# First inverse FFT step in parts of 32 rows by 64 columns, with a scratch layout ordered by k1

## The chip, the cores and the metric

The kernel runs on one core of a Trainium2 chip. Its time is the device time of one execution in microseconds. Three runs of the kernel before gave 374.64, 375.82 and 376.35 us, with a median of 375.82 us. The profiled execution took 376.04 us; its trace, from the first to the last instruction, spans 374.1 us.

Five engines run side by side, each working through its own instructions in order: TensorE (PE, matrix products; PEld is its weight load), VectorE (DVE), ScalarE (ACT), GpSimd (POOL) and SyncE (SP, which here only issues DMA transfers). DMA transfers are issued from SP, ACT and POOL and are carried by 16 DMA engines.

## The reference

The input has 2048 positions (S) of 448 channels (D). The result is a sum of three terms: the input, a gated long convolution, and a two-layer MLP.

```python
xn = layernorm(q)
k_shift = causal depthwise conv of k with 4 taps
kv = k_shift * v
y  = irfft(rfft(kv, 2S) * rfft(ssm_k, 2S))[:S] + kv * ssm_D   # a causal convolution of length S per channel
A  = xn * y
B  = mish(xn @ w1 + b1) @ w2                                   # 448 -> 1792 -> 448
out = q + A + B
```

## The kernel before

**Two strands on one PE.** The MLP and the convolution share every engine. The host code is a list of 116 slots. Each slot holds a piece of the MLP: even slots a first-layer group (`g1_mm`, L462, pairs of 128 hidden units for a chunk of 256 positions), odd slots the Mish and the split of its result into two parts (`mish`, L470, L73, L74) and a second-layer group (`g2_mm`, L487 to L489). The parts of the convolution are put into slots by hand: `at(slot, ...)` places a piece ahead of the slot's MLP work, `after(slot, ...)` behind it. No scheduler moves anything afterwards, so this list is the order on every engine.

**The convolution as products.** Each channel's 2048 samples are written as n = n2 + 32 n1, with 32 values of n2 and 64 of n1. A forward transform is one product over n1 (`f1_mm`, L124, result to the scratch tensors `Dh` and `Dkv` in DRAM) and one over n2 (`f2_mm`, L198). The 64 values of k1, the index that goes with n1, are treated in eight octets `o`; within one, k1 is given by t (4 values) and r (2 values). Per octet the spectra are multiplied on DVE (`prod`, L231, result `ya` real and `yc` imaginary). The first inverse step (`i1_mm`, L243) takes k2 back to n2: for each (t, r) the 32 rows of k2, real (c = 0) and imaginary (c = 1), are multiplied by the constant `gi`, with the two c summed in PSUM. `i1_out` copies the two PSUM tiles to `qe` on ACT (L251) and stores `qe` to the DRAM scratch `E` (L255, from SP). An octet comes every third slot from slot 69 to slot 90.

**The second inverse step.** It works on chunks of positions. `e_load(c)` (L278) brings chunk c of `E` into a tile `e` of 128 partitions, for the two halves h of k1 (octets 0 to 3 and 4 to 7). `fold(c)` forms the sum `ex` and the difference of the halves on DVE (L283, L285), `i2_mm(c)` (L301) takes k1 back to n1, and `gate` multiplies by the normalised input. Chunks 6 and 7 come first: their loads are issued from SP, at slot 94, their folds stand behind slot 95, their products ahead of slot 98. The loads of the other six chunks are issued from POOL. Four buffers hold `e`, so the loads of chunks 2 to 5 wait until an earlier chunk's product has read its buffer.

**Tiles of the PE.** All convolution products use parts of the 128 by 128 array: f1 has 32 rows by 64 columns, f2 64 by 32, i1 32 by 32 and i2 64 by 32. Each of these float32 products shows in the trace as two weight loads and two matmuls.

Of the kernel before, what the change touches and what calls it, by code (L numbers as in the profile page):

```python
# [7 lines left out]
F32 = mybir.dt.float32  # L8
# [6 lines left out]
S, D, F = 2048, 448, 1792  # L15
# [4 lines left out]
NCHUNK = S // CH  # L20
# [8 lines left out]
I2_AT = {98: (6, 7), 102: (0, 1), 106: (2, 3), 109: (4, 5)}  # L29
# [6 lines left out]
def tile_kernel(ctx: ExitStack, tc, q, k, v, sk, hT, sD, w1, b1, w2, c_f1, c_g, c_gi, c_i2, out):  # L36
    nc = tc.nc
    V = nc.vector

    def pool(name, bufs=1, stack=ctx, **kw):  # L40
        return stack.enter_context(tc.tile_pool(name=name, bufs=bufs, **kw))
# [7 lines left out]
    dp = pool("scratch", space=DRAM)  # L49
# [2 lines left out]

    Dh = dp.tile([NO * 16, 32, D], F32, name="Dh")
    Dkv = dp.tile([NO * 16, 32, D], F32, name="Dkv")
    E = dp.tile([2, 2, 32, 2, NCHUNK, 2, D], F32, name="E")

    f1id = cp.tile([128, 2, 128], F32, name="f1id")
    f1, ident = f1id[:, 0], f1id[:, 1]
# [17 lines left out]
    def pc():  # L76
        return pcp.tile([128, 2, 512], F32, name="pc")
# [93 lines left out]
    GT, AH, AV, HS, PV, Y = {}, {}, {}, {}, {}, {}  # L171

    def t2(shape, name, bufs=1):
        if not sp2:
            ph1.close()
            sp2.append(ph2.enter_context(tc.tile_pool(name="ph2", bufs=1, reuse_waits="tile")))
        return sp2[0].tile(shape, F32, name=name, bufs=bufs)
# [56 lines left out]
    def i1_mm(o):  # L234
        gi = GT[o][1]
        ps = [pc(), pc()]
        for c in range(2):
            for t in range(4):
                ts = slice(32 * t, 32 * t + 32)
                for r in range(2):  # L240
                    for jj in range(2):
                        cg = 64 * jj + 32 * r
                        nc.tensor.matmul(ps[t // 2][cg:cg + 32, t % 2, :D], gi[ts, r, c, 32 * jj:32 * jj + 32],  # L243
                                         Y[o][c][ts, r], start=c == 0, stop=c == 1, tile_position=(32 * t, cg))
        PS["I", o] = ps
        Y.pop(o)

    def i1_out(o):
        qe = t2([128, 4, D], "qe")
        for i, p in enumerate(PS.pop(("I", o))):  # L250
            nc.scalar.copy(qe[:, 2 * i:2 * i + 2], p[:, :, :D])  # L251
        k = 8 * (o % 4)
        for jj in range(2):
            dst = E[o // 4, jj, k:k + 8].rearrange("(t r) m j b d -> (r m j b) t d", t=4)
            nc.sync.dma_start(dst, qe[64 * jj:64 * jj + 64])  # L255


    ph3 = ExitStack()
# [3 lines left out]
    def t3(shape, name, bufs=2):  # L262
        if not sp3:
            ph2.close()
            sp3.append(ph3.enter_context(tc.tile_pool(name="ph3", bufs=2, reuse_waits="tile")))
            i2 = sp3[0].tile([128, 2, 32], F32, name="i2", bufs=1)
            nc.sync.dma_start(i2, c_i2)
            sp3.append(i2)
        return sp3[0].tile(shape, F32, name=name, bufs=bufs)
# [4 lines left out]
    def e_load(c):  # L274

        e = EE[c] = t3([128, 2, 2, D], "e3", 4)
        src = E[:, :, :, :, c].rearrange("h j k m b d -> (j k m) h (b d)")
        (nc.sync if c in I2_AT[min(I2_AT)] else nc.gpsimd).dma_start(e.rearrange("p h b d -> p h (b d)"), src)  # L278

    def fold(c):  # L280
        e = EE[c]
# [267 lines left out]
    for g, t in enumerate(KV_AT):  # L549
        d = t - (KV_AT[g - 1] if g else t - 6)  # L550
# [16 lines left out]
    for o in range(NO):  # L567
        s, d = OCT_AT[0] + OCT_AT[1] * o, OCT_AT[1]
        h = s - 1 if o else H0_AT
        at(h - d if o else h - 2, o_load, AH, Dh, o, "ah")  # L570
        at(s - d if o else s - 2, o_load, AV, Dkv, o, "av")
        at(h, h2_mm, o)
        after(h, h2_out, o)
        at(s, v2_mm, o)
        after(s, v2_out, o)
        at(s, gi_load, o)
        after(s + 1, prod, o, 0)
        after(s + 2, prod, o, 1)
        at(s + 4, i1_mm, o)
        after(s + 4, i1_out, o)  # L580

    ts = sorted(I2_AT)
    for n, t in enumerate(ts):
        for m, c in enumerate(I2_AT[t]):
            at(ts[n - 2] + 1 if n > 1 else ts[0] - 4 + n, e_load, c)
            at(ts[n - 1] + (2 if m else -2 if n == 2 else -1) if n > 1 else ts[0] - 5 + m, qa_load, c)
            after(t - 3, fold, c)
            at(t, i2_mm, c)
            after(t, gate, c)
            at(t + 2 + m, gate_out, c)  # L590
# [30 lines left out]
    ps = [g2p.tile([128, 512], F32, name="pg2") for _ in range(2)]  # L621
# [11 lines left out]
    for s in range(nslots):  # L633
        j = s // 2 - G2_LAG - 1
# [11 lines left out]
def _constants():  # L646
    import numpy as np

    w = lambda e: np.exp(-2j * np.pi * (np.asarray(e) % 8192) / 8192.0)

    n1 = np.arange(64)
    k1 = np.arange(64)
    W = w(32 * n1[:, None] * (4 * k1[None, :] - 1))

    W = W.reshape(32, 2, 64).transpose(1, 0, 2).reshape(64, 64)
    Wo = W.reshape(64, 8, 2, 4).transpose(0, 1, 3, 2)
    f1 = np.stack([Wo.real, Wo.imag], axis=4).reshape(64, 128)
    f1 = np.concatenate([f1, f1])

    i2 = np.stack([W.real.T, W.imag.T], axis=1)[:32].reshape(4, 2, 4, 2, 64).transpose(0, 2, 1, 3, 4).reshape(64, 2, 32) / 2048  # L660
    i2 = np.concatenate([i2, i2])
    n2 = np.arange(32)[:, None] // 2 + 16 * (np.arange(32)[:, None] % 2)
    k2 = np.arange(32)[None, :]
    G = np.zeros((2, 2, 32, 8, 4, 2, 32))
    GI = np.zeros((4, 32, 8, 2, 2, 2, 2, 8, 2))
    for kk in range(64):
        o, r, t = kk // 8, kk // 4 % 2, kk % 4
        g = w(n2 * (4 * kk - 1) + 256 * n2 * k2)
        G[r, 0, :, o, t, 0], G[r, 1, :, o, t, 0] = g.real, -g.imag
        G[r, 0, :, o, t, 1], G[r, 1, :, o, t, 1] = g.imag, g.real  # L670

        gt = g.T.reshape(32, 8, 2, 2).transpose(0, 2, 1, 3)
        GI[t, :, o, r, 0, :, 0], GI[t, :, o, r, 1, :, 0] = gt.real, gt.imag
        GI[t, :, o, r, 0, :, 1], GI[t, :, o, r, 1, :, 1] = -gt.imag, gt.real
    c = lambda a: np.ascontiguousarray(a, dtype=np.float32)
    return dict(c_f1=c(np.stack([f1, np.eye(128)], axis=1)), c_g=c(G.reshape(128, 8, 4, 2, 32)), c_gi=c(GI.reshape(128, 8, 2, 2, 64)),
                c_i2=c(i2))
# [27 lines left out]
```

## Time and profile before

| | |
|---|---|
| profiled execution | 376.04 us, span 374.1 us |
| PE busy | 366.6 us, 98% of the span |
| DVE, ACT, POOL busy | 266.1, 177.4, 23.1 us |
| i1 products (L243) | 512 matmuls, two for each product |
| stores of `E` (L255, SP) | 16 of 448 KB, median 5.5 us to landing |
| loads of `e` (L278) | 2 of 896 KB from SP, 6 from POOL |
| granted PE clock | 1.00 in nearly all stretches |

Busy time of a matmul group is that of overlapping records, so the length of a PE piece is better read from the start of its first matmul to the start of the next group. Idle time is put down to the engine or transfer that ended it. A trace row's first number is the start in us from the beginning of the span, the second its length.

### The profile page before, as it was taken

Reading aid. Unit: us, or ns where it says so; the run is one execution under the profiler, and the core shown is the slowest. Engines: PE = TensorE matmul, PEld = TensorE weight load, DVE = VectorE, ACT = ScalarE, POOL = GpSimd, SP = SyncE. Lnnn points to the kernel's source line nnn. Section 1 sums busy time; section 2 is a strip of 40 time slices with the busy share of each in tenths; the row PEclk is TensorE's granted clock in tenths of the full one; section 3 lists DMA queues with packets and bytes.
Section 4 is the critical chain, followed back from the end, with each engine's and each line's share of the span. In section 5 each row is a group of like instructions: output and inputs, shape, how many; then the busy total and the mean of one; then the engine's idle time right before and its main releaser. Section 6 shows DMA issues by size and latency. Waiting matters only on the chain.

```text
span 374.1 us, 7973 instructions
## 1 busy us (share of the span) xinstructions
PE 366.6 (98%) x3392; PEld 295.6 (79%) x3392; DVE 266.1 (71%) x356; ACT 177.4 (47%) x298; POOL 23.1 (6%) x40
## 2 busy tenths in 40 slices
PE   8999999999999999999999999999999999999995
PEld 3887888888888988988886666666666889789884
DVE  5798758999999998996444746754664823797841
ACT  4777553542436333533454745556555436135450
POOL 2010001000020001000000000110000011102110
PEclk9999999999999999999999999999999999999999
DMA  8899979747587436604794598879394459839973
GB/s 283 296 314 324 390 284 271 182 157 224 156 271 217 98 86 212 197 2 123 236 298 152 145 299 228 261 240 263 110 296 145 116 129 330 304 112 279 230 139 90
DMA packets 32099, 79.38 MB, mean 212 GB/s; under 512 B 2881, under 2 KB 18114, under 8 KB 32066
## 3 DMA queue, kind: packets, MB, share of 16 engines
q1 hardware_dynamic: 25442, 55.56, 46.3%
q10 hardware_dynamic: 4896, 15.08, 14.8%
q0 software_dynamic: 1728, 8.26, 8.3%
q8 instruction: 26, 0.43, 0.4%
q14 instruction: 7, 0.06, 0.1%
HBM read 50.44 MB, written 28.44 MB: 211 GB/s over the span
## 4 chain that ended last, share of the span: by engine, by line
PE 80%; DVE 9%; DMA 5%; ACT 3%; issue 2%; POOL 0%; SPq 0%; ACTq 0%; DVEq 0%
PE pg L462 32%; PE pg L487 10%; PE pg L488 10%; PE pg L489 10%; PE pc L198 7%; PE pc L243 4%; PE pc L124 3%; PE pc L301 2%; PE pg L423 2%; DMA kr<-in_k_dram 2%; DMA Dkv<-st 1%; DMA av<-Dkv 1%; DVE st L131 1%; DVE bst L379 1%; DVE acl L74 1%
## 5 line engine op out<-in xcount | busy, mean ns | idle before, releaser
L470 ACT ACTIVATE a<-pg,b1t 128x256 f32<-128x256 f32 x112 | 47.2, 473 | 108.7 <-PE pg L462 90.1
L462 PE MATMUL pg<-XH,w1h 128*128 128x256 f32 x448 | 91.2, 285 | 0.3 <-DVE XL L433 0.2
L487 PE MATMUL pg<-w2h,ach 128*128 128x448 f32 x224 | 83.6, 373 | 0.2 <-DVE qt L494 0.2
L462 PEld LDWEIGHTS pg<-XH,w1h 128*128 128x128 f32 x448 | 69.7, 188 | 17.5 <-issue 14.4
L488 PE MATMUL pg<-w2l,ach 128*128 128x448 f32 x224 | 81.3, 363 | 0.4 <-DVE w2l L74 0.4
L489 PE MATMUL pg<-w2h,acl 128*128 128x448 f32 x224 | 81.3, 363 | 0.0
L74 DVE TENSOR_TENSOR acl<-a,ach 128x512 fp32r<-128x512 f32 x56 | 38.5, 687 | 57.9 <-ACT ach L73 57.6
L462 PE MATMUL pg<-XL,w1h 128*128 128x256 f32 x448 | 69.7, 277 | 0.0
L462 PEld LDWEIGHTS pg<-XL,w1h 128*128 128x128 f32 x448 | 59.5, 188 | 0.1
L462 PE MATMUL pg<-XH,w1l 128*128 128x256 f32 x336 | 56.9, 278 | 0.0
L487 PEld LDWEIGHTS pg<-w2h,ach 128*128 128x128 f32 x224 | 42.0, 187 | 14.1 <-issue 11.2
L462 PEld LDWEIGHTS pg<-XH,w1l 128*128 128x128 f32 x336 | 47.0, 188 | 0.0
L488 PEld LDWEIGHTS pg<-w2l,ach 128*128 128x128 f32 x224 | 42.1, 188 | 3.0 <-DVE w2l L74 0.7
L489 PEld LDWEIGHTS pg<-w2h,acl 128*128 128x128 f32 x224 | 42.1, 188 | 2.7
L73 ACT CAST ach<-a 128x512 fp32r<-128x512 f32 x56 | 34.9, 623 | 1.8
L162 DVE TENSOR_TENSOR x<-x 128x896 f32<-128x896 f32 x24 | 26.2, 1091 | 0.8
L435 ACT CAST XH<-pg 128x512 fp32r<-128x512 f32 x16 | 9.4, 589 | 28.0 <-PE pg L423 28.0
L433 DVE TENSOR_TENSOR XL<-pg,XH 128x512 fp32r<-128x512 f32 x16 | 10.9, 685 | 14.9 <-ACT XH L435 14.8
L130 ACT COPY st<-pc 128x896 f32<-128x896 f32 x16 | 14.5, 908 | 13.3 <-PE pc L124 13.3
L131 DVE TENSOR_TENSOR st<-pc,st 128x896 f32<-128x896 f32 x16 | 17.4, 1086 | 4.5 <-ACT st L130 4.1
L251 ACT COPY qe<-pc 128x896 f32<-128x896 f32 x16 | 13.7, 911 | 13.4 <-PE pc L243 13.4
L390 POOL TENSOR_TENSOR shift<-mv,mone 128x2 f32<-128x2 f32 x7 | 2.8, 394 | 281.0 <-DVE mv L382 281.0
(65 smaller groups left out, 397.0 us busy)
## 6 DMA issues: line engine op xcount, KB each, us to landing
Dh<-st ACTq DMA_DIRECT2D x16, 448.0 KB, 5.5
Dkv<-st ACTq DMA_DIRECT2D x16, 448.0 KB, 4.9
ah<-Dh SPq DMA_DIRECT2D x8, 896.0 KB, 7.1
av<-Dkv SPq DMA_DIRECT2D x8, 896.0 KB, 6.1
E<-qe SPq DMA_DIRECT2D x16, 448.0 KB, 5.5
e<-E POOLq DMA_DIRECT2D x6, 896.0 KB, 8.4
kr<-in_k_dram SPq DMA_DIRECT2D x10, 448.0 KB, 6.1
x<-in_hT_dram SPq DMA_DIRECT2D x8, 448.0 KB, 6.8
```

The costliest lines, as they stand in the source:

```text
L73: nc.scalar.copy(h, raw)
L74: V.tensor_sub(l, raw, h)
L130: nc.scalar.copy(st[:, 1], o)
L131: V.tensor_add(st[:, 0], e, st[:, 1])
L162: V.tensor_add(KV[g], KV[g], o)
L198: nc.tensor.matmul(p[32 * t:32 * t + 32, r, :D], g[rs, t, c], a[rs, t], start=True, stop=True, tile_position=(64 * r, 32 * t))
L243: nc.tensor.matmul(ps[t // 2][cg:cg + 32, t % 2, :D], gi[ts, r, c, 32 * jj:32 * jj + 32], Y[o][c][ts, r], start=c == 0, stop=c == 1, tile_ ...
L462: nc.tensor.matmul(ps[:, n], l, r, start=n_ == 0, stop=n_ == len(mm) - 1)
L470: nc.scalar.activation(a[:, n], ps[:, n], AF.Mish, bias=b1t[:, 2 * p + n:2 * p + n + 1])
L487: nc.tensor.matmul(ps, ah[:, n, cs], w2h[:, f], start=f == 0, stop=False)
L488: nc.tensor.matmul(ps, ah[:, n, cs], w2l[:, f], start=False, stop=False)
L489: nc.tensor.matmul(ps, al[:, n, cs], w2h[:, f], start=False, stop=f == NF - 1)
```

## The change

Five places change. `E` gets the order (half h, 32 values of k1, m for real and imaginary part of the result, j for even and odd n2, chunk, b, channel) in place of (h, j, k1, m, chunk, b, channel). The constant `gi` has its 64 columns in the order (m, j, chunk, b) in place of (j, m, chunk, b). `i1_mm` makes one product of 64 columns where it made two of 32, so an octet has 16 products in place of 32, and the output partitions are grouped by r alone. `i1_out` still makes two stores of 448 KB for an octet; each now takes all 128 partitions of `qe` for two values of t, where it took 64 partitions for all four. `e_load` makes two loads of 448 KB, one for each half h, where it made one of 896 KB. On the DRAM side such a load has 2 values of j on the outside and then 64 rows of 3584 B; on the on-chip side it has 128 partitions of 3584 B. Before, both sides had 128 on the outside.

```diff
-    E = dp.tile([2, 2, 32, 2, NCHUNK, 2, D], F32, name="E")
+    E = dp.tile([2, 32, 2, 2, NCHUNK, 2, D], F32, name="E")
...
             for t in range(4):
                 ts = slice(32 * t, 32 * t + 32)
                 for r in range(2):
-                    for jj in range(2):
-                        cg = 64 * jj + 32 * r
-                        nc.tensor.matmul(ps[t // 2][cg:cg + 32, t % 2, :D], gi[ts, r, c, 32 * jj:32 * jj + 32],
-                                         Y[o][c][ts, r], start=c == 0, stop=c == 1, tile_position=(32 * t, cg))
+                    nc.tensor.matmul(ps[t // 2][64 * r:64 * r + 64, t % 2, :D], gi[ts, r, c], Y[o][c][ts, r],
+                                     start=c == 0, stop=c == 1, tile_position=(32 * t, 64 * r))
...
-        for jj in range(2):
-            dst = E[o // 4, jj, k:k + 8].rearrange("(t r) m j b d -> (r m j b) t d", t=4)
-            nc.sync.dma_start(dst, qe[64 * jj:64 * jj + 64])
+        dst = E[o // 4, k:k + 8].rearrange("(t r) m j c b d -> (r m j c b) t d", t=4)
+        for i in range(2):
+            nc.sync.dma_start(dst[:, 2 * i:2 * i + 2], qe[:, 2 * i:2 * i + 2])
...
-        src = E[:, :, :, :, c].rearrange("h j k m b d -> (j k m) h (b d)")
-        (nc.sync if c in I2_AT[min(I2_AT)] else nc.gpsimd).dma_start(e.rearrange("p h b d -> p h (b d)"), src)
+        src = E[:, :, :, :, c].rearrange("h k m j b d -> h j (k m) (b d)")
+        for h in range(2):
+            (nc.sync if c in I2_AT[min(I2_AT)] else nc.gpsimd).dma_start(e[:, h].rearrange("p b d -> p (b d)"), src[h])
...
-        GI[t, :, o, r, 0, :, 0], GI[t, :, o, r, 1, :, 0] = gt.real, gt.imag
-        GI[t, :, o, r, 0, :, 1], GI[t, :, o, r, 1, :, 1] = -gt.imag, gt.real
+        GI[t, :, o, r, 0, 0], GI[t, :, o, r, 1, 0] = gt.real, gt.imag
+        GI[t, :, o, r, 0, 1], GI[t, :, o, r, 1, 1] = -gt.imag, gt.real
```

The changed kernel's line numbers are two lower from `i1_mm` on (L243 is L241) and one lower from the loads of `e` on (L278 is L277).

On PE, the first octet's inverse step (slot 69) stands between a first-layer and a second-layer group. Before:

```order
L462 MATMUL pg_2342<-XL,w1h 128x256 x4
L243 MATMUL pc<-ya,gi 32x448 x16
L243 MATMUL pc<-yc,gi 32x448 x16
L487 MATMUL pg_2067<-w2h,ach 128x448
L488 MATMUL pg_2067<-w2l,ach 128x448
```

With the change (a row's size is output partitions by columns, its count is of products):

```order
L461 MATMUL pg_2342<-XL,w1h 128x256 x4
L241 MATMUL pc<-ya,gi 64x448 x8
L241 MATMUL pc<-yc,gi 64x448 x8
L486 MATMUL pg_2067<-w2h,ach 128x448
L487 MATMUL pg_2067<-w2l,ach 128x448
```

The place is the same, with half as many products, each twice as wide in its output.

On SP, the stores of the last octet (`E<-qe`) are followed by the constant of the second inverse step, the input of a chunk, and the loads of chunks 6 and 7. Before:

```order
L255 DMA E<-qe 64x4x448 x2
L267 DMA i_3607<-in_c_i_dram 128x64
L292 DMA q_3609<-in_q_dram 128x896
L278 DMA e_3630<-E 128x2x896
L278 DMA e_3632<-E 128x2x896
L292 DMA q_3634<-in_q_dram 128x896
```

With the change:

```order
L253 DMA E<-qe 128x2x448 x2
L265 DMA i_3479<-in_c_i_dram 128x64
L291 DMA q_3481<-in_q_dram 128x896
L277 DMA e_3502<-E 128x1x896 x2
L277 DMA e_3505<-E 128x1x896 x2
L291 DMA q_3508<-in_q_dram 128x896
```

Each of the two loads has become two of half the size in the same place; the size shown is that of the on-chip side.

On DVE, whose order has not changed, the folds of chunks 6 and 7 stand between two splits of MLP results (`acl`):

```order
L74 TENSOR_TENSOR acl<-a,ach 128x512
L282 TENSOR_TENSOR ex<-e_3502 128x896
L284 TENSOR_TENSOR e_3502<-e_3502 128x896
L282 TENSOR_TENSOR ex<-e_3505 128x896
L284 TENSOR_TENSOR e_3505<-e_3505 128x896
L432 TENSOR_TENSOR XL<-pg_3576,XH 128x4x128
L74 TENSOR_TENSOR acl<-a,ach 128x512
```

What stands behind them is a part of the next chunk's MLP input (`XL`) and the next split, which wait on DVE until the folds have been done.

## Prediction

> **What bounds the kernel now.** I read the page's busy times and the chain that ended last, then the list of waits, then the timeline around the places that the change touches.
>
> ```profile
> PE 366.6 (98%) x3392; PEld 295.6 (79%) x3392; DVE 266.1 (71%) x356; ACT 177.4 (47%) x298; POOL 23.1 (6%) x40
> PE 80%; DVE 9%; DMA 5%; ACT 3%; issue 2%; POOL 0%; SPq 0%; ACTq 0%; DVEq 0%
> ```
>
> The PE is busy for 98% of the span and makes up 80% of the chain: PE time saved is time saved, and whatever stops the PE is added in full. Its waits on the second inverse step are short:
>
> ```profile
> DVE ex L283 <- DMA e<-E: 2.3, 1, 2.3
> PEld pc L301 <- DVE e L285: 0.8, 1, 0.8
> SPq L278 <- DMA E<-qe: 1.1, 1, 1.1
> ```
>
> Once, a fold on DVE waited 2.3 us for a load of `e`, and the PE then 0.8 us for that fold. So one place has no slack: the first use of `E`.
>
> **Part 1: the products of the first inverse step.** Pieces of the PE timeline, one of each kind and what follows it:
>
> ```profile
> 234.56 1.03 PE L243 MATMUL pc<-ya,gi 32*32 32x448 f32 x32
> 235.33 1.36 PE L243 MATMUL pc<-yc,gi 32*32 32x448 f32 x32
> 236.62 0.47 PE L487 MATMUL pg<-w2h,ach 128*128 128x448 f32 x1
> ...
> 212.47 1.74 PE L198 MATMUL pc<-ah,g 64*32 64x448 f32 x32
> 214.14 0.62 PE L462 MATMUL pg<-XH,w1h 128*128 128x256 f32 x3
> ...
> 22.87 1.01 PE L124 MATMUL pc<-x,f1id 32*64 32x448 f32 x16
> 23.81 0.47 PE L487 MATMUL pg<-w2h,ach 128*128 128x448 f32 x1
> ```
>
> An octet's inverse step holds the PE for 236.62 - 234.56 = 2.06 us. Its 64 matmuls sit on 16 parts of the array, so it is four rounds; the first two (`ya`) take 0.77 us, the last two (`yc`), which add to the same PSUM, take 1.29. The changed step has 32 matmuls on 8 parts, four rounds again. Two rows are near. f2 also has 32 matmuls on 8 parts: 214.14 - 212.47 = 1.67 us. f1 has exactly the new shape, 16 matmuls in 0.94 us, so twice that, 1.88 us, is an upper end that counts the finish twice. No row shows the new shape adding to PSUM. If that is what holds `yc` back, the step stays at 2.06 us. So the gain per octet lies between 0 and 0.39 us; I take 0.39, since f2 has the same count and the same number of parts: 8 x 0.39 = 3.1 us over eight octets.
>
> **Part 2: the stores of `E`.**
>
> ```profile
> L251 ACT COPY qe<-pc 128x896 f32<-128x896 f32 x16 | 13.7, 911 | 13.4 <-PE pc L243 13.4
> L278 POOL DMA_DIRECT2D e<-E x6: 722/724/927, 310.2 to 336.7; - x6
> ```
>
> Bytes, number, queue and piece size (1792 B) stay. The first store of an octet now needs one ACT copy in place of both, so it starts some 0.9 us sooner (the copy takes 911 ns); the last still follows the second copy. Only the last octet's landing is waited for (1.1 us on SP above). I count nothing, with 1 us either way.
>
> **Part 3: the loads of `e`.** Twelve loads in place of six on POOL cost six more issues of 0.72 to 0.93 us on an engine that is 6% busy: nothing. The shape is what matters. All transfers of the kernel before but one have 64 or 128 on the outside on both sides; the new loads have 2 on the DRAM side. What would that do? The page counts packets:
>
> ```profile
> DMA packets 32099, 79.38 MB, mean 212 GB/s; under 512 B 2881, under 2 KB 18114, under 8 KB 32066
> q10 hardware_dynamic: 4896, 15.08, 14.8%
> q0 software_dynamic: 1728, 8.26, 8.3%
> Dh<-st ACTq DMA_DIRECT2D x16, 448.0 KB, 5.5
> ...
> i<-in_c_i_dram SPq DMA_DIRECT2D x1, 32.0 KB, 3.6
> b1t<-in_b_dram SPq DMA_DIRECT2D x1, 7.0 KB, 5.2
> x<-in_sD_dram SPq DMA_DIRECT2D x1, 1.8 KB
> ```
>
> The ACT queue q10 carries 34 transfers (32 stores and 2 loads) of 128 pieces: 4352 packets. It has 4896, so each transfer has 16 more, one for each engine as I read it. Over all queues there are 165 transfers from the first row of the list to the last. Of the 2881 packets under 512 B, 256 are data (128 of 56 B of `b1t`, 128 of 256 B of `i`); the other 2625 are 164 x 16 + 1. So one transfer has a single closing packet, and one row, that of the one-row `sD`, has no landing time. I read from this that a transfer with 1 on the outside went to one engine, those with 64 or 128 to sixteen. The new loads lie between: on sixteen engines if the 128 of the on-chip side counts, on two if the 2 does. An outer count of 2 is nearer to the 1 than to the 64, and I take two engines for the loads from SP. The four have one shape and one queue, and nothing in them points to different engines, so I put them on the same two; no row can show that.
>
> The Trainium skill states the rule outright ("DMA: Bandwidth & Descriptors", section "Why a DMA increments its semaphore by 16 and not by 1"): the number of engines is the largest up to 16 that divides the slowest dimension of both sides; on SP's queue these are the lowest-numbered ones. By it the four loads from SP would share the same two engines, and the time would be the one forecast below; for POOL's queue the skill has the choice move round, which would add no stall. The trace agrees as far as its one-row transfer goes.
>
> What it costs:
>
> ```profile
> core 0: us, PE busy (x) PEld busy (x) DVE busy (x) ACT busy (x) POOL busy (x), PEclk, DMA share, GB/s
> 309.40:321.40 12.00, 12.00 (x84) 11.57 (x83) 4.17 (x5) 6.61 (x13) 1.68 (x2) 1.00 0.96 362
> 315.00:320.00 5.00, 5.00 (x38) 4.82 (x37) 3.36 (x4) 2.10 (x5) 0.00 (x0) 1.00 1.02 414
> 309.37 0.89 SPq L278 DMA_DIRECT2D e<-E  x2
> out_dram<-qt SPq DMA_DIRECT2D x4, 224.0 KB, 2.5
> ```
>
> While chunks 6 and 7 were loaded, the engines were 0.96 busy at 362 GB/s: 362 / 0.96 / 16 = 23.6 GB/s for one. In the busiest 5 us it is 25.4. The four loads from SP are 4 x 458,752 = 1.835 MB, 917.5 KB on each of two engines: 38.9 us (36.1 at the higher rate) in place of 4.9. They start at 309.37, less the 3.1 us of part 1, so at 306.3. A 224 KB store lands in 2.5 us, of which its bytes need 0.6, so 1.9 us come on top. Chunk 6 is there after half the bytes, near 328, chunk 7 at 306.3 + 1.9 + 38.9 = 347.1. POOL's loads of chunks 0 and 1 (1.835 MB), spread over sixteen engines, put 115 KB on the same two: up to 4.9 us, of which I take half: 349.5.
>
> ```profile
> 316.28 0.69 DVE L74 TENSOR_TENSOR acl<-a,ach 128x512 fp32r<-128x512 f32 x1 [0.71 <-ACT ach L73]
> 316.89 1.08 DVE L283 TENSOR_TENSOR ex<-e 128x896 f32<-128x896 f32 x1
> 318.01 1.09 DVE L285 TENSOR_TENSOR e<-e 128x896 f32<-128x896 f32 x1
> 321.41 1.09 DVE L283 TENSOR_TENSOR ex<-e 128x896 f32<-128x896 f32 x1 [2.31 <-DMA e<-E]
> 322.54 1.09 DVE L285 TENSOR_TENSOR e<-e 128x896 f32<-128x896 f32 x1
> 323.55 0.68 DVE L433 TENSOR_TENSOR XL<-pg,XH 128x512 fp32r<-128x512 f32 x1
> ...
> 322.00 0.57 PE L301 MATMUL pc<-ex,i 64*32 64x448 f32 x2
> 323.68 0.57 PE L301 MATMUL pc<-e,i 64*32 64x448 f32 x2
> 324.58 0.62 PE L462 MATMUL pg<-XH,w1h 128*128 128x256 f32 x3
> ```
>
> DVE works in order: behind the two folds stand `XL` and the next `acl`, so the MLP gets no input past them. The PE works in order too: both products of L301 stand ahead of the MLP group at 324.58. Before, chunk 7's fold began when its load landed (321.41) and the PE took its result at 323.68, 2.27 us later. Now that is 349.5 + 2.3 = 351.8, so everything from there on moves by 351.8 - 323.68 = 28.1 us. This already holds the 3.1 us of part 1: they only let the loads start sooner. Chunks 2 to 5 follow from POOL with their waits moved along; chunks 0 and 1 land during the stall.
>
> One more term: the PE stands still for some 10 us and then 20 us. At the start, the first matmuls after rest were slow:
>
> ```profile
> L601 PE MATMUL pc<-one 128*16 128x448 f32 x8 | 5.4, 841 | 1.0 <-DVE one L595 1.0
> L124 PE MATMUL pc<-x,f1id 32*64 32x448 f32 x256 | 16.5, 560 | 0.0
> ```
>
> 841 ns against 560 for the same 448 columns. Such a restart after the stall costs between nothing and the 5.4 us of that warm-up; I take 2.
>
> **Sum.** The profiled execution took 376.04 us, 1.94 more than its span and 0.2 above the median of 375.82. 376.04 + 28.1 + 2 = 406.1: I forecast 406 us. Its own range: without sharing and clock loss and at 25.4 GB/s, chunk 7 lands at 344.3 and the time is 399; with full sharing (2.5 more), 5.4 us of restart and no gain in part 1 it is 415.
>
> **Rivals.**
>
> *Sixteen engines after all.* If the on-chip side's 128 decides, the loads run as before: each engine moves 56 KB for a chunk, in one load or in two. Then only part 1 is left: 376.0 - 3.1 = 372.9 us, faster. For it: POOL and SP loads of 128 partitions today all have sixteen closing packets. Against it: all of them have 64 or more on both sides.
>
> *Sixteen engines and no gain.* The `yc` rounds take 0.52 us more than the `ya` rounds for the same number of matmuls; if adding to PSUM does that, the step stays at 2.06 us and the time at 376.
>
> *POOL's loads pile up as well.* If the twelve loads from POOL use one pair of engines of their own, each pays 9.7 us in a row. Chunks 0 and 1 (38.9 us from about 308) are done by 347, chunk 2 by 366 and chunk 3 by 386, where DVE wants it near 366; chunks 4 and 5 end at 425, some 28 us later than wanted after that. With both stalls the time is about 406 + 20 + 28 = 454 us. For it: the same shape. Against it: the profile lists POOL's queue as software and the others as hardware, and no row shows how it chooses.
>
> *Two engines, but another pair for each load.* Then a load lands in about 1.9 + 9.7 = 11.6 us and chunk 7 near 319 to 322, as before; the time is that of the first rival, and its chance is counted there.
>
> **Chances.** Two engines, one pair: 0.66. Sixteen, or spread, with the gain of part 1: 0.20. The same without it: 0.08. Pile-up on POOL too: 0.06. About 0.5% is what a measurement of this kernel can tell from no change. Faster by more than that takes nearly all of the second case, 0.18; slower is the first and the last and a little of the third, 0.73; within 0.5%: 0.09. Both signs are likely, so the range goes from 371 to 416 us, which takes in the forecast's own 399 to 415 and the cases at 373 and 376; 454 is left out.
>
> **What would show it.** The loads of `e` have no landing time in the list of transfers, like `sD`, and the count of small packets falls: four loads from SP bring 8 closing packets where two brought 32. DVE waits some 10 us for chunk 6 and some 20 more for chunk 7, and the PE waits on L301 for the folds. The DMA share around 310 to 350 falls far below 0.96 while the stall lasts. An octet's step on PE takes 1.67 us where it took 2.06. I am wrong if the loads land in under 10 us, or if the PE goes past the products of chunks 6 and 7 without a wait of 15 us or more.

## The result and the profile after

The changed kernel takes 413.77 us (median of 4 runs, 412.91 to 414.14) against 375.88 us before: a ratio of 1.1004 with a 95% interval of 1.0982 to 1.1026. The forecast was 406 us, its own range 399 to 415. The profiled execution took 414.14 us and spans 412.2 us. All ratios below are to the kernel before, run beside the kernel in question. Of the kernels below, e5, e6 and e13 had one execution each of over 700 us, which is left out and not explained here; in e6 it was the profiled one, so of its profile only the packet counts are used.

The page of the changed kernel, with the engines, the chain of work that ended last, and its packet counts:

```profile
PE 366.8 (89%) x3136; PEld 294.4 (71%) x3136; DVE 266.7 (65%) x356; ACT 177.2 (43%) x298; POOL 28.5 (7%) x46
PE 78%; DMA 11%; DVE 5%; ACT 3%; SPq 1%; issue 1%; POOL 0%; DVEq 0%
DMA packets 37547, 79.40 MB, mean 193 GB/s; under 512 B 8329, under 2 KB 23562, under 8 KB 37514
```

The PE has 256 matmuls fewer, but its share of the span fell from 98% to 89%, and transfers take 11% of the chain where they took 5%. The timeline says where. First DVE, with its idle time in brackets, and its row in the list of waits; then PE:

```profile
313.69 0.69 DVE L74 TENSOR_TENSOR acl<-a,ach 128x512 fp32r<-128x512 f32 x1 [0.70 <-ACT ach L73]
334.52 1.09 DVE L282 TENSOR_TENSOR ex<-e 128x896 f32<-128x896 f32 x1 [20.14 <-DMA e<-E]
335.65 1.09 DVE L284 TENSOR_TENSOR e<-e 128x896 f32<-128x896 f32 x1
356.74 1.09 DVE L282 TENSOR_TENSOR ex<-e 128x896 f32<-128x896 f32 x1 [20.00 <-DMA e<-E]
DVE ex L282 <- DMA e<-E: 41.7, 3, 20.1
...
335.67 1.70 PE L300 MATMUL pc<-ex,i 64*32 64x448 f32 x4 [16.18 <-DVE ex L282]
357.89 1.71 PE L300 MATMUL pc<-ex,i 64*32 64x448 f32 x4 [19.36 <-DVE ex L282]
359.01 0.96 PE L300 MATMUL pc<-e,i 64*32 64x448 f32 x2
```

The fold of chunk 6 waits 20.1 us for its load, that of chunk 7 another 20.0, and the PE waits behind each. Two stretches of 10 us out of the stall, from the view of stretches (PE busy at the start of a row; clock, DMA share and GB/s at its end):

```profile
320.00:330.00 10.00, 0.00 (x0) 0.00 (x0) 0.00 (x0) 0.00 (x0) 0.00 (x0) 0.73 0.14 54
330.00:340.00 10.00, 2.86 (x16) 0.40 (x16) 2.18 (x2) 0.00 (x0) 1.13 (x2) 0.50 0.13 51
```

A share of 0.13 is two engines of sixteen, and 51 GB/s is 25.5 for each of them. The list of transfers, as answered for the loads and stores of `E`:

```profile
E<-qe SPq DMA_DIRECT2D x16, 448.0 KB, 3.6
e<-E POOLq DMA_DIRECT2D x12, 448.0 KB, 15.3
e<-E SPq DMA_DIRECT2D x4, 448.0 KB
```

SP's loads have no landing time, like the one-row `sD`. As a sign this is weak: POOL's loads have one, and in this run `f1id` and `b1t`, whose shape did not change, have lost theirs (3.4 and 5.2 us before). The products did get shorter:

```profile
233.70 1.01 PE L241 MATMUL pc<-ya,gi 32*64 32x448 f32 x16
234.50 0.96 PE L241 MATMUL pc<-yc,gi 32*64 32x448 f32 x16
235.39 0.47 PE L486 MATMUL pg<-w2h,ach 128*128 128x448 f32 x1
```

An octet's step takes 235.39 - 233.70 = 1.69 us in place of 2.06.

### The profile page after: what moved, and what is told of

Same layout as the page of the kernel before. It is cut to its first block, busy times and chain, and to the rows that moved or that the text cites. A ratio compares the mean times of both kernels' runs of the same rounds, so it can differ in the third digit from the quotient of the medians.

```text
span 412.2 us, 7491 instructions
## 1 busy us (share of the span) xinstructions
PE 366.8 (89%) x3136; PEld 294.4 (71%) x3136; DVE 266.7 (65%) x356; ACT 177.2 (43%) x298; POOL 28.5 (7%) x46
## 2 busy tenths in 40 slices
DMA packets 37547, 79.40 MB, mean 193 GB/s; under 512 B 8329, under 2 KB 23562, under 8 KB 37514
## 4 chain that ended last, share of the span: by engine, by line
PE 78%; DMA 11%; DVE 5%; ACT 3%; SPq 1%; issue 1%; POOL 0%; DVEq 0%
PE pg L461 33%; PE pg L486 10%; PE pg L488 9%; PE pg L487 9%; DMA e<-E 9%; PE pc L198 7%; PE pc L124 3%; PE pc L241 3%; PE pc L300 2%; PE pg L422 2%; DMA kr<-in_w_dram 2%; SPq L277 1%; ACT a L469 1%; DMA qt<-in_q_dram 1%; DVE bst L378 1%
## 5 line engine op out<-in xcount | busy, mean ns | idle before, releaser
L300 PE MATMUL pc<-ex,i 64*32 64x448 f32 x64 | 10.9, 644 | 35.5 <-DVE ex L282 35.5
L282 DVE TENSOR_TENSOR ex<-e 128x896 f32<-128x896 f32 x8 | 8.7, 1087 | 41.7 <-DMA e<-E 41.7
L300 PEld LDWEIGHTS pc<-ex,i 64*32 64x32 f32 x64 | 2.1, 114 | 39.5 <-DVE ex L282 37.4
```

Source lines behind the costliest of these rows:

```text
L300: nc.tensor.matmul(p[cg:cg + 32, jj, :D], sp3[1][rs, h], e[h][rs, b], start=True, stop=True, tile_position=(64 * jj, cg))
```

## The experiments

**Is it the form of the loads, and which part of it?** Four kernels of one chip. The first keeps the changed kernel and cuts its loads by j:

```diff
-        src = E[:, :, :, :, c].rearrange("h k m j b d -> h j (k m) (b d)")
-        for h in range(2):
-            (...).dma_start(e[:, h].rearrange("p b d -> p (b d)"), src[h])
+        for jj in range(2):
+            src = E[:, :, :, jj, c].rearrange("h k m b d -> (k m) h (b d)")
+            (...).dma_start(e[64 * jj:64 * jj + 64].rearrange("p h b d -> p h (b d)"), src)
```

> The changed kernel with its loads of e cut by j instead of by h: each load is 64 rows by 2 halves on both sides, same bytes, same number, same layout of E. Theory (outer count): 64 on the outside on both sides means sixteen engines, so the loads land in under 12 us, the stall on chunks 6 and 7 goes, and the 0.37 us per octet that the trace of the changed kernel shows for the products is left: 373 us (371.5 to 374.5). Rival (layout): if the reading of E in its new order is what is slow, the same rows are read and the time stays at 405 to 415. Rival (more and smaller loads): it also stays above 385.

Measured: 381.13 us, ratio 1.0122 (1.0093 to 1.0151). The stall of 40 us is gone, so neither the order of `E` nor the number of loads made it. But 8 us more are left than expected, a miss: chunk 7's fold still waits 9.5 us.

The second is the kernel before with its loads cut by h, with 128 rows on the outside:

```diff
-        src = E[:, :, :, :, c].rearrange("h j k m b d -> (j k m) h (b d)")
-        (...).dma_start(e.rearrange("p h b d -> p h (b d)"), src)
+        src = E[:, :, :, :, c].rearrange("h j k m b d -> h (j k m) (b d)")
+        for h in range(2):
+            (...).dma_start(e[:, h].rearrange("p b d -> p (b d)"), src[h])
```

> The kernel before with its loads of e cut by h into two of 448 KB, 128 rows on the outside on both sides. Theory (outer count): sixteen engines, as before; 376 us (375 to 378). Rival (more and smaller loads): the number of loads and their size are those of the changed kernel, so the loads of chunks 6 and 7 land late and the time is above 385.

Measured: 374.92 us, ratio 0.9968 (0.9954 to 0.9981). Twice as many loads of half the size cost nothing.

The third adds a gap to `E` behind each block of j, and nothing else but the same cut:

```diff
-    E = dp.tile([2, 2, 32, 2, NCHUNK, 2, D], F32, name="E")
+    E = dp.tile([2, 2, 33, 2, NCHUNK, 2, D], F32, name="E")
...
+        src = E[:, :, 0:32, :, c].rearrange("h j k m b d -> h j (k m) (b d)")
+        for h in range(2):
+            (...).dma_start(e[:, h].rearrange("p b d -> p (b d)"), src[h])
```

> The kernel before with loads cut by h, and E with one unused row of k1 behind each block of j, so that the 128 rows of a load no longer form one run of equal steps but 2 blocks of 64. Products, stores and order of E stay as before. Theory (outer count): two engines; chunk 7 lands 45 to 55 us after the first load is issued, no landing times for SP's loads; 410 to 422 us. Rival (layout ordered by k1) and rival (more and smaller loads): 376 to 380.

Measured: 419.93 us (417.48 to 420.36), ratio 1.1157 (1.1129 to 1.1184). An unused row in a scratch tensor, with the products, the stores and the order of `E` of the kernel before, costs 43.8 us. The packet counts of the two pages, in all and of the queues of SP (q1) and POOL (q0), first with the 128 rows in one run (e4), then in 2 blocks of 64 (e5):

```profile
DMA packets 32228, 79.38 MB, mean 213 GB/s; under 512 B 3009, under 2 KB 18242, under 8 KB 32194
q1 hardware_dynamic: 25474, 55.56, 46.7%
q0 software_dynamic: 1824, 8.26, 8.4%
...
DMA packets 37548, 79.43 MB, mean 191 GB/s; under 512 B 8329, under 2 KB 23562, under 8 KB 37514
q1 hardware_dynamic: 25418, 55.56, 42.3%
q0 software_dynamic: 7200, 8.30, 8.6%
```

Eight loads more than before are 8 x 16 closing packets: 2881 + 128 = 3009 in e4. On SP's queue 56 packets go, as they must if each of its four loads has 2 closing packets in place of 16. The rest of the difference, 8329 - 3009 + 56 = 5376, is all on POOL's queue: 12 x 448, and 448 = 14 x 32. So I read that for each load from POOL the fourteen engines that carry no data get 32 small packets each, half as many as an engine with data has rows.

The fourth leaves POOL's loads as changed and cuts only SP's by j, by the edit of e1 under a condition.

> The changed kernel with only SP's loads (chunks 6 and 7) cut by j, POOL's twelve left as they are. Theory (the stall is that of SP's four loads on one pair of engines): chunks 6 and 7 arrive within 14 us, POOL's loads take 10 to 16 us on pairs that move round and have that slack; 373 to 380 us. Rival (POOL's loads stall as well): chunks 2 to 5 come late and the time stays above 390.

Measured: 388.05 us, ratio 1.0304 (1.0274 to 1.0335), a miss. The folds of chunks 6 and 7 still wait 6.2 and 8.8 us, that of chunk 4 1.0. POOL's loads do not stall by themselves; but beside them, and with the cut of e1, SP's loads stay late.

**Does the number of engines follow the outer count?** As e5, with 4 blocks of 32 rows (the tile is `[2, 4, 17, 2, ...]`) and 8 blocks of 16 (`[2, 8, 9, 2, ...]`).

> As e5, but each load's 128 rows in E lie in 4 blocks of 32 rows with a gap behind each. Theory (engines follow the outer count of the DRAM side): four engines, so half the bytes of e5 on each; chunk 7, which took 53 us from the first issue in e5, takes some 25 to 29, and the time is near 390 (384 to 396). Rival (any load whose rows are not one run of equal steps is slow): as e5, near 420.

> As e5, but in 8 blocks of 16 rows. Theory (engines follow the outer count): eight engines; chunk 7 takes 13 to 16 us from the first issue, 376 to 380 us. Rival (not one run of equal steps): near 420.

Measured: e6 took 401.34, 407.56 and 408.63 us, e7 393.77 us, ratio 1.0445 (1.0404 to 1.0485). Both are above what I expected: 2, 4, 8 blocks and one run give 420, 401 to 409, 394 and 375 us. The counts of e6 and e7:

```profile
DMA packets 34484, 79.40 MB, mean 110 GB/s; under 512 B 5265, under 2 KB 20498, under 8 KB 34450
...
DMA packets 32964, 79.39 MB, mean 205 GB/s; under 512 B 3745, under 2 KB 18978, under 8 KB 32930
```

With four engines the rule of e5 gives 3009 - 4 x 12 + 12 x 12 x 16 = 5265, with eight 3009 - 4 x 8 + 12 x 8 x 8 = 3745. Both are exact, and so is the part on SP's queue, with 48 and 32 packets fewer than in e4. The number of engines follows the outer count of the DRAM side; the time follows it in order, but not in size. What holds e7 back is in its stretches:

```profile
313.00:318.00 5.00, 5.00 (x37) 4.80 (x36) 1.38 (x2) 2.53 (x5) 0.00 (x0) 1.00 1.02 205
```

All sixteen engines are busy (1.02), with 205 GB/s; in the kernel before the same stretch has 398 (below). Why each engine is slower there was not tried.

**Why did e1 not gain?** The kernel before with its loads cut by j, so that each goes to 64 of the 128 partitions:

```diff
...
+        for jj in range(2):
+            src = E[:, jj, :, :, c].rearrange("h k m b d -> (k m) h (b d)")
+            (...).dma_start(e[64 * jj:64 * jj + 64].rearrange("p h b d -> p h (b d)"), src)
```

> The kernel before with its loads cut by j, each into 64 partitions of e, E and its order as before. It tells why e1 lost 5 us against the kernel before instead of gaining 3. Theory (a transfer that touches only 64 of the 128 partitions runs at little over half the rate): chunk 7 lands some 20 us after the first issue and DVE waits 8 us or more for it, 380 to 388 us. Rival (it was the order of E, whose rows for one j lie 56 KB apart and not 28): 375 to 377 us.

Measured: 385.05 us, ratio 1.0230 (1.0193 to 1.0268). The folds of chunks 6 and 7 wait 4.6 and 6.2 us. The stretch while chunks 6 and 7 are loaded, in the kernel before and in e9:

```profile
313.00:318.00 5.00, 5.00 (x37) 4.79 (x37) 2.39 (x3) 2.54 (x5) 0.00 (x0) 1.00 1.01 398
...
313.00:318.00 5.00, 5.00 (x37) 4.79 (x36) 1.38 (x2) 2.54 (x5) 0.00 (x0) 1.00 1.01 214
```

The engines are as busy, but move 214 GB/s in place of 398. `E` is in its old order, so the order is not the cause, and e4 rules out the number of loads. What is left is the cut by j, by which a load writes 64 partitions; it also reads other rows of `E` together, and no run takes the two apart. Nor are all 128 partitions enough: e7 writes them from eight engines and has 205 GB/s.

**The products alone.** The change's products, `gi` and `E` as before, and four stores of 32 partitions for an octet:

```diff
...
+        for r in range(2):
+            for jj in range(2):
+                dst = E[o // 4, jj, k:k + 8].rearrange("(t r) m j b d -> r (m j b) t d", t=4)
+                nc.sync.dma_start(dst[r], qe[64 * r + 32 * jj:64 * r + 32 * jj + 32])
```

> The change's products alone (parts of 32 rows by 64 columns, both n2 in one), with E and its loads as before; the stores of an octet become four of 32 partitions. Theory: 0.37 us per octet on PE, 3.0 us in all, nothing lost on the loads: 373 us (372 to 374.5). Rival (the gain is lost where the loads of chunks 6 and 7 are waited for, or to four stores in place of two on SP): 376 or more.

Measured: 372.67 us, ratio 0.9898 (0.9869 to 0.9928). Its folds wait 1.5 us in all for loads, the PE 0.3 for a fold, and PE busy time falls with the span:

```profile
PE 363.4 (98%) x3136; PEld 293.9 (79%) x3136; DVE 266.0 (72%) x356; ACT 177.0 (48%) x298; POOL 23.2 (6%) x40
E<-qe SPq DMA_DIRECT2D x32, 224.0 KB, 3.5
DVE ex L282 <- DMA e<-E: 1.5, 1, 1.5
PEld pc L300 <- DVE ex L282: 0.3, 1, 0.3
```

This is the faster version: the change without its new order of `E`. With the loads cut by h on top of it:

> The change's products with E ordered as before (e8) and the loads cut by h with 128 rows on the outside (e4). Theory (the two small gains add, since one is PE time and the other an earlier landing of chunk 6 and 7): 371 to 372.5 us. Rival (the load for chunk 7 is hidden anyway once the products are faster): as e8, 372.7 us.

Measured: 372.86 us, ratio 0.9922 (0.9904 to 0.9941). The two gains do not add; the rival holds.

**Why was chunk 7 later than forecast?** First POOL's loads cut by j, SP's left as changed.

> The changed kernel with only POOL's loads cut by j (16 engines); SP's four loads stay with 2 on the outside. Chunk 7 came 7 us later in the changed kernel than forecast. Theory (POOL's loads took turns with SP's on the shared pair of engines): without them there chunk 7 arrives near 345 to 350 us and the time is 403 to 408 us. Rival (SP's loads are that slow on two engines by themselves): 411 to 416 us.

Measured: 414.14 us, ratio 1.1021 (1.0998 to 1.1045), a miss for the theory as posed. But e1 and e9 show that this cut makes POOL's loads hold all engines for longer, so it may have taken little away (10.1 us to landing in both, 6.2 in e4). Then POOL's loads of chunks 0 and 1 left out:

```diff
+        if c in (0, 1):
+            nc.gpsimd.memset(e.rearrange("p h b d -> p (h b d)"), 0.0)
+            return
```

> The changed kernel without POOL's loads of chunks 0 and 1 (their tiles are set to zero, so the convolution is left out of the output for these 512 positions). SP's four loads with 2 on the outside stay, and nothing from POOL shares their engines during the stall. In e3 those POOL loads ran on sixteen engines but slowly, so they may still have cost the pair as much. Theory (other traffic on the pair makes chunk 7 late): chunk 6 arrives near 324, chunk 7 near 343 to 347 us, and the time is 399 to 405 us. Rival (SP's loads are that slow on two engines by themselves): chunk 7 near 356, 411 to 416 us.

Measured: 411.04 us (409.06 to 411.66), ratio 1.0942 (1.0889 to 1.0996). The time is the rival's, but the trace is not. DVE's folds, the issue of the loads on SP, a stretch while they run, and POOL's first loads:

```profile
323.40 1.09 DVE L285 TENSOR_TENSOR ex<-e 128x896 f32<-128x896 f32 x1 [9.33 <-DMA e<-E]
352.21 1.09 DVE L285 TENSOR_TENSOR ex<-e 128x896 f32<-128x896 f32 x1 [26.58 <-DMA e<-E]
302.51 16.88 SPq L280 DMA_DIRECT2D e<-E  x4
305.00:320.00 15.00, 14.18 (x97) 13.32 (x95) 2.08 (x3) 7.08 (x14) 2.60 (x2) 1.00 0.13 51
327.78 1.87 POOL L280 DMA_DIRECT2D e<-E  x2 [20.17 <-PE pc L303]
```

With POOL quiet, two engines are all that runs (0.13), and chunk 6 arrives at 323.4, just where 302.5 + 1.9 + 19.4 = 323.8 puts it; in the changed kernel it was 334.5. Then chunk 6's buffers come free, POOL issues the loads of chunk 2 at 327.8, and chunk 7 takes 28.8 us more in place of 19.4. So SP's pair of engines has the rate that I took, and what makes the chunks late is the other traffic during it.

The packets of the two queues tell which traffic. In the changed kernel, from 320 to 324 us, then from 326 to 338, and last SP's alone from 310 to 324 (packets, MB, share of sixteen engines):

```profile
q0 software_dynamic: 27, 0.18, 11.0%
q1 hardware_dynamic: 18, 0.06, 4.1%
...
q1 hardware_dynamic: 170, 0.60, 12.3%
q0 software_dynamic: 170, 0.00, 0.8%
...
q1 hardware_dynamic: 65, 0.23, 4.2%
```

While POOL's data runs, SP's queue moves 18 packets in 4 us. Afterwards, with as many small packets from POOL as its own beside it, it moves 170 in 12 us, or 57 in 4. So POOL's data holds SP's loads up, and its small packets do not; the next loads of `q` were not issued before 330.7. Over the whole stretch from 310 to 324 SP moves 65 packets where 198 would have gone at the later rate, which is 9.4 us lost; in e13 chunk 7 loses 28.8 - 19.4 = 9.4 us as well. One load of 448 KB on two engines takes 9.7 us at the rate that I took. I read from this that one of POOL's loads stood on SP's own pair; no view names the engines.

## Why the prediction was right

**The mechanism.** Part 3 chose two engines for a load with 2 on the outside, from one odd closing packet in 2625. The packet counts on SP's queue (56, 48 and 32 fewer for 2, 4 and 8 blocks, and 56 fewer than in e4 in the changed kernel too) bear it out to the last packet, and e5 shows that this alone makes the loss. The Trainium skill's rule ("DMA: Bandwidth & Descriptors", section "Why a DMA increments its semaphore by 16 and not by 1") gave the same number; the counts agree for SP. For POOL it has the engines move round, which no view here shows directly; POOL's data on 46.3% of sixteen engines from 312 to 318 us, while its four loads ran, is 7.4 engines and so more than one pair.

**Part 1, the products.** 1.67 us per octet forecast, 1.69 measured; 372.9 us for the change without the stall, 372.67 measured in e8. Adding to PSUM is not by itself what held `yc` back: in the new shape the `yc` rounds add as well, and the two parts now take 0.80 and 0.89 us. What held them back on sixteen parts is open.

**Part 2, the stores.** Here the term was too small. I counted nothing, with 1 us either way. The loads are issued at 302.48, 6.9 us before the old 309.37, of which part 1 explains 3.1. The stores land in 3.6 us in place of 5.5, and SP is done with its two in 1.17 us, where it took 2.85:

```profile
299.65 1.17 SPq L253 DMA_DIRECT2D E<-qe  x2
302.48 28.16 SPq L277 DMA_DIRECT2D e<-E  x4
```

**Part 3, the size.** Chunk 7 arrived at 356.7, not 349.5, although its load started 3.8 us earlier, so the loads took 11 us longer than my sum. The rate of an engine was right: 25.5 GB/s against the 23.6 I took. The step that failed is the sharing, for which I had 2.4 us and 4.9 at most. It rested on POOL's loads lying on sixteen engines, or moving round without a stall. They had two each as well, their data held SP's queue down to a third of its rate (18 packets in 4 us against 57), and e13 shows chunk 6 on time once they are away. Of the delay against a pair that SP has alone, 334.5 - 323.8 = 10.7 us fall on chunk 6 and 2.8 more on chunk 7; the 2.8 are not taken apart.

**Restart of the PE.** The product of chunk 7's difference starts at 359.01 in place of 323.68, 35.3 us later; the span is 38.1 longer. 2.8 us remain, and 2 was my term for the restart. The next second-layer group behind this product, before and after:

```profile
327.21 0.36 PE L487 MATMUL pg<-w2h,ach 128*128 128x448 f32 x1
...
363.99 0.36 PE L486 MATMUL pg<-w2h,ach 128*128 128x448 f32 x1
```

The way there takes 363.99 - 359.01 = 4.98 us where it took 327.21 - 323.68 = 3.53, at a granted clock of 0.50 up to 362. This is 1.45 of the 2.8; the other 1.35 are not taken apart.

**The sum.** 28.1 + 2 forecast, 35.3 + 2.8 measured: 7.2 us of the miss of 7.8 are the sharing net of the earlier start. That 413.8 still lies within 399 to 415 is in part luck. The upper end was made of 2.5 us more of sharing, 5.4 us of restart and no gain in part 1. What came was 13.5 us of sharing in all, of which an earlier start hid 3.8, with a small restart and the full gain.

**The rivals.** Sixteen engines: refuted by e5 and the counts; its number, 372.9, is what the products alone give. No gain from the products: refuted by e8. Another pair for each load: refuted by e13, where two engines are all that is busy (0.13) while SP issues its four loads. A pile-up on POOL that stalls chunks 2 to 5: not seen, DVE waits for loads three times, 20.1, 20.0 and 1.6 us. The signs that I named (no landing time, a fallen DMA share, both waits) came, the first of them on transfers of other shapes too. Small packets rose by 5448 instead of falling, for POOL's loads add them.

## What to carry to other kernels

Write down for each transfer what stands on the outside of both access patterns, and write rows at equal steps as one dimension where the layout allows it: here 2 in place of 128 took a load from sixteen engines to two and cost 44 us (e5), with no other sign in the code. A change of a product's shape is worth taking alone, with the layout that the next reader wants left as it is: the products gave 1.0%, the layout that was meant to go with them took 11%. And a load on a path where the PE waits must be costed with the traffic that runs beside it.

## What the runs showed of the hardware that was not expected

**Busy engines at half the rate.** With loads cut into 64 of 128 partitions, all engines ran at 1.01 of their time for 214 GB/s, against 398 with 128 (e9 and before). Loads into all 128 from eight engines each were as slow (1.02 and 205, e7). The Trainium skill has a rule that two transfers to disjoint halves of the partitions are not worth it since they share the same engines ("DMA: Bandwidth & Descriptors", section "Rules for kernel authors"); here the engines were shared, and each of them was slower as well. The stores of `E` point the same way: 5.5 us to landing from 64 partitions, 3.6 from 128 for the same bytes.

**A queue that blocks.** With loads on two engines each in the changed kernel, SP spent 28.16 us in issuing four of them, where two large ones had taken 0.89; by the same timeline the load of `q` behind them was not issued before 330.7.

**Small packets.** A load from POOL on k engines brings packets under 512 B beyond its sixteen closing ones: 448 for k = 2, 192 for k = 4, 64 for k = 8, by the counts above. That they belong to the engines that it does not use is my reading. SP's loads kept their full rate beside them.

**The clock in a stall.** The granted clock was 0.73 from 320 to 330 us and 0.50 from 330 to 340, and the way back cost 1.45 us on the PE behind the stall.
